# An adaLN block with a spectral filter: the column transform factored into 128 and five points

## The chip, the cores and the metric

The kernel runs on one core of a Trainium2 chip. The metric is device time in microseconds (us) of one execution; the kernel before takes 278.77 us (median of three runs, 278.70 to 280.73). The engines are TensorE (PE; its weight loads are shown apart as PEld), VectorE (DVE), ScalarE (ACT), GpSimd (POOL) and SyncE (SP), whose queue issues nearly all DMAs here.

## The reference

x is 2048 x 640 (bf16, called A_x). w_r and w_i are 2048 x 321, w_mod is 640 x 3840, c is 1 x 640; the feed-forward weights are 640 x 1728 (twice) and 1728 x 640.

```python
mod = (silu(c) @ w_mod).reshape(1, 6, 1, -1)
sa, ca, ga, sb, cb, gb = (mod[:, i] for i in range(6))
h = layernorm(x) * (1 + ca) + sa                  # over the 640 columns, eps 1e-5
X = rfft2(h.astype(float32), axes=(-2, -1))       # 2048 x 321, complex
y = irfft2(X * (w_r + 1j * w_i), s=(2048, 640)).astype(bfloat16)
x = x + ga * y
h = layernorm(x) * (1 + cb) + sb
x = x + gb * ((silu(h @ w_gate) * (h @ w_up)) @ w_down)
```

## The kernel before, in words

Row index s = 16 p + t (p: partition, 128; t: 16 tiles), and frequency k = 128 k2 + k1. All transforms are matmuls with tables (R for the columns, G for the 128 points of the rows, K for the 16 points over t; H, K, Rinv back). The order of the work is written out by hand; each engine runs its instructions in program order and waits on semaphores.

**Stage 1** (lines 270 to 416), for each tile t, in the order of the string `plan`: row statistics on VectorE (`ln1_half`, L280; `ln1_aggr`, L283), the root on ScalarE (L251) and its reciprocal (L289), `ln1_xn` (the normalised row, L293); `turn`, five transposes of 128 columns, even columns, odd columns and a mixed block (L301); `turned`, the copy to SBUF as hT (L305); `dfwd`, 2 x 3 matmuls of 328 columns with the table Rs = R(1 + ca), for even and odd columns (L309); `zcopy` (L318); `s1`, four matmuls of 328 columns with the G table (L332, L333); `acopy` to A_sb (L343), laid out in groups of four column frequencies, so that one group is 128 wide (t, complex part, four frequencies). The evictions are dealt out to VectorE and ScalarE by the lists HT_DVE, Z_DVE and A_DVE.

**Stage 2** (lines 419 to 609) runs over 11 units of four groups. Each group is turned so that (t, part, four) lies on the partitions: the first three units by TensorE (`t2`), the others by a DMA transpose that SP issues (`transposed`). Then `stage_a`, the 16-point transform, combines the even and odd halves E and O into the frequency l and its mirror 320 - l (L463, L464), with an eviction to X (L466) and an add of the transform of sa at row frequency 0 on GpSimd (L469); `product` with the weights Wb and the mirrored Wq (L479); `stage_b`, a transpose by matmul that also adds the two complex products (L488); `evict_y` (L496, L498); `stage_c`, the inverse 16 points (L512, L513), evicted to Ep (L519). The weights of the mirrored frequencies are read through a DRAM scratch tensor, Wneg, which turns the row order; `negate` makes the negative planes on VectorE (L360). `epx` and the fold of the gate ga into Rinv (L586) stand between the units.

**Stage 3** (lines 666 to 712), for each t: `s1inv`, ten matmuls of 128 columns (L673 to L679); the copies to VT (L681, L682); `dinv`, six matmuls of 320 columns with Rinv (L689), and x1 = x + that, two adds of 320 columns on VectorE (L692). Statistics and normalisation of the first four tiles for the second layernorm run between them.

**Feed-forward part** (from L720), four blocks of 512 rows: 13 x 10 matmuls of 512 columns and a rest (`gu13`), Silu on ScalarE (L741), product on VectorE (L742), then the product with w_down (L770, L775) and the output. The fold of gb into w_down (L751) runs in the first block.

Of the kernel before, what the change touches and what calls it, by code (L numbers as in the profile page):

```python
# [18 lines left out]
LH = 164  # L19
L = 2 * LH  # L20
NG = 41
LP = 2 * NG
LW = 324
NC5 = 5
NFC = 14
# [3 lines left out]

_ROWS = np.concatenate([np.arange(0, 512, 2), np.arange(512, 640), np.arange(1, 512, 2)])


# [3 lines left out]
def _tables():  # L41
# [3 lines left out]
    l = np.arange(161, dtype=np.float64)[None, :]  # L45
    ang = 2.0 * np.pi * ((_ROWS[:, None] * l) % D) / D
    R = np.zeros((D, 2, LH))
    R[:, 0, 0:161] = np.cos(ang)
    R[:, 1, 0:161] = np.where(l == 0, 0.0, -np.sin(ang))
    R = R.reshape(NC5, P, L)  # L50
    even = np.arange(P)[:, None] % 2 == 0
    R6 = np.stack([R[0], R[1], np.where(even, R[2], 0.0), np.where(even, 0.0, R[2]), R[3], R[4]])
    T["R"] = np.ascontiguousarray(R6.transpose(1, 0, 2)).astype(_NPBF)
    p = np.arange(P, dtype=np.float64)[:, None]
    k1 = np.arange(128, dtype=np.float64)[None, :]
    G = np.zeros((P, NT, 3, 128))
    for t in range(NT):
        a = 2.0 * np.pi * ((k1 * (16 * p + t)) % S) / S
        G[:, t, 0, :] = np.cos(a)
        G[:, t, 1, :] = -np.sin(a)  # L60
        G[:, t, 2, :] = np.sin(a)
    T["G"] = G.astype(_NPBF)
    kk = np.arange(128, dtype=np.float64)[:, None]
    pp = np.arange(P, dtype=np.float64)[None, :]
    H = np.zeros((128, NT, 3, P))
    for t in range(NT):
        a = 2.0 * np.pi * ((kk * (16 * pp + t)) % S) / S
        H[:, t, 0, :] = np.cos(a)
        H[:, t, 1, :] = np.sin(a)
        H[:, t, 2, :] = -np.sin(a)  # L70
    T["H"] = H.astype(_NPBF)

    F16 = np.exp(-2j * np.pi * np.outer(np.arange(16), np.arange(16)) / 16)

    def fwd(F, turn):
        M = np.zeros((16, 2, 4, 2, 16, 4))
        for j in range(4):
            i = 3 - j if turn else j
            M[:, 0, j, 0, :, i] = F.real
            M[:, 1, j, 0, :, i] = -F.imag  # L80
            M[:, 0, j, 1, :, i] = F.imag
            M[:, 1, j, 1, :, i] = F.real
        return M.reshape(128, 128)

# [51 lines left out]
def adaln_block_kernel(  # L136
# [85 lines left out]
    for i in range(2):  # L222
        nc.sync.dma_start(Wq[:, i], Wneg[i])
# [626 lines left out]
```

## Time and profile before

| | us |
|---|---|
| median of 3 runs | 278.77 |
| the profiled execution's own time | 279.14 |
| its span, first to last instruction | 277.4 |
| TensorE busy | 267.5 (96%) |
| VectorE busy | 162.6 (59%) |
| ScalarE busy | 112.7 (41%) |
| GpSimd busy | 8.9 (3%) |
| granted TensorE clock, mean | 0.998 |

Matmuls are pipelined, and a busy TensorE is not one at its peak. A group's mean is the duration of one instruction; where instructions follow each other without a wait, their starts lie closer together than their durations. The idle time of an engine that is not the bottleneck costs nothing.

### The profile page before, as it was taken

Reading aid. Unit: us, or ns where it says so; the run is one execution under the profiler, and the core shown is the slowest. Engines: PE = TensorE matmul, PEld = TensorE weight load, DVE = VectorE, ACT = ScalarE, POOL = GpSimd, SP = SyncE. Lnnn points to the kernel's source line nnn. Section 1 sums busy time; section 2 is a strip of 40 time slices with the busy share of each in tenths; the row PEclk is TensorE's granted clock in tenths of the full one; section 3 lists DMA queues with packets and bytes.
Section 4 is the critical chain, followed back from the end, with each engine's and each line's share of the span. In section 5 each row is a group of like instructions: output and inputs, shape, how many; then the busy total and the mean of one; then the engine's idle time right before and its main releaser. Section 6 shows DMA issues by size and latency. Waiting matters only on the chain.

```text
span 277.4 us, 5268 instructions
## 1 busy us (share of the span) xinstructions
PE 267.5 (96%) x2120; PEld 168.3 (61%) x2120; DVE 162.6 (59%) x411; ACT 112.7 (41%) x220; POOL 8.9 (3%) x31
## 2 busy tenths in 40 slices
PE   6899989999899999999999999999999999999995
PEld 5667768998687844446654445664444764444663
DVE  4899966799499738876327854224872242432132
ACT  5899666999454662322022233004233103223000
POOL 1000013311000000000000000000000000000000
PEclk9999999999999999999999999999999999999999
DMA  7989999699994200050110050021013011000011
GB/s 260 413 225 211 355 324 194 186 266 397 363 381 95 39 21 24 0 97 0 50 52 16 0 94 3 1 72 33 9 26 70 1 71 35 11 0 0 2 47 47
DMA packets 41034, 31.16 MB, mean 112 GB/s; under 512 B 29361, under 2 KB 37810, under 8 KB 40882
## 3 DMA queue, kind: packets, MB, share of 16 engines
q1 hardware_dynamic: 41008, 30.83, 39.3%
q8 instruction: 16, 0.26, 0.4%
q14 instruction: 8, 0.07, 0.1%
q10 hardware_dynamic: 2, 0.00, 0.0%
HBM read 22.96 MB, written 3.93 MB: 97 GB/s over the span
## 4 chain that ended last, share of the span: by engine, by line
PE 86%; DVE 7%; DMA 2%; ACT 2%; issue 1%; SPq 0%; ACTq 0%; DVEq 0%
PE gps L738 20%; PE ups L738 20%; PE oa L775 10%; PE ob L775 10%; PE zps L309 3%; PE yps L488 3%; DMA Rp<-tab_R 2%; PE xps L463 2%; PE oa L689 2%; PE xps L464 2%; PE gu L725 2%; DVE st L280 2%; PE ob L689 1%; DVE x_sb L692 1%; PE t1ps L301 1%; PE aps L332 1%
## 5 line engine op out<-in xcount | busy, mean ns | idle before, releaser
L738 PE MATMUL gps<-h2T_all,Wg 128*128 128x512 bf16 x260 | 64.6, 379 | 0.0
L738 PE MATMUL ups<-h2T_all,Wu 128*128 128x512 bf16 x260 | 64.6, 379 | 0.0
L741 ACT ACTIVATE sg<-gps 128x512 f32<-128x512 f32 x52 | 31.0, 597 | 74.0 <-PE gps L738 72.3
L738 PEld LDWEIGHTS <-Wu 128*128 128x128 bf16 x260 | 25.4, 98 | 30.7
L738 PEld LDWEIGHTS <-Wg 128*128 128x128 bf16 x260 | 25.4, 98 | 30.5
L742 DVE TENSOR_TENSOR ATb<-ups,sg 128x512 bf16<-128x512 f32 x26 | 17.9, 690 | 32.0 <-PE ups L738 32.0
L742 DVE TENSOR_TENSOR ATa<-ups,sg 128x512 bf16<-128x512 f32 x26 | 17.9, 688 | 20.4 <-PE ups L738 17.5
L775 PEld LDWEIGHTS <-ATa 128*128 128x128 bf16 x208 | 20.2, 98 | 8.8 <-issue 0.8
L775 PEld LDWEIGHTS <-ATb 128*128 128x128 bf16 x208 | 20.2, 98 | 8.6 <-issue 0.5
L785 DVE TENSOR_TENSOR xo<-oa,x_sb 128x320 bf16<-128x320 f32 x16 | 7.8, 489 | 29.7 <-PE ob L770 22.2
L728 ACT ACTIVATE sg<-gu 64x512 f32<-64x512 f32 x4 | 2.3, 586 | 45.3 <-PE gu L725 45.3
L775 PE MATMUL oa<-Wd_sb,ATa 128*128 128x320 bf16 x104 | 15.6, 299 | 0.0
L775 PE MATMUL oa<-Wd_sb,ATb 128*128 128x320 bf16 x104 | 15.5, 299 | 0.0
L775 PE MATMUL ob<-Wd_sb,ATb 128*128 128x320 bf16 x104 | 15.4, 299 | 0.0
L775 PE MATMUL ob<-Wd_sb,ATa 128*128 128x320 bf16 x104 | 15.4, 299 | 0.0
L309 PE MATMUL zps<-Rs,hT 128*128 128x328 bf16 x90 | 14.8, 303 | 0.2
L280 DVE BATCH_NORM_STATS2 st<-x_sb 128x6 f32<-128x320 bf16 x32 | 13.8, 469 | 0.8 <-DMA x_sb<-in_A_x_dram 0.8
L785 DVE TENSOR_TENSOR xo<-ob,x_sb 128x320 bf16<-128x320 f32 x16 | 7.8, 487 | 10.2 <-PE ob L775 10.2
L681 ACT CAST VT<-va 128x512 bf16<-128x512 f32 x16 | 9.4, 586 | 8.0 <-PE va L677 6.2
L488 PE MATMUL yps<-identb,PP 128*128 128x128 bf16 x162 | 11.5, 219 | 0.6 <-DVE PP L479 0.4
L309 PEld LDWEIGHTS <-hT 128*128 128x128 bf16 x96 | 8.8, 98 | 5.2 <-ACT hT L305 1.0
L466 ACT CAST X<-xps 128x512 bf16<-128x512 f32 (+1 forms) x21 | 11.2, 598 | 1.6 <-PE xps L464 1.6
(207 smaller groups left out, 412.8 us busy)
## 6 DMA issues: line engine op xcount, KB each, us to landing
out_dram<-xo SPq DMA_DIRECT2D x16, 160.0 KB, 1.8
Wg<-in_B_w_gate_dram SPq DMA_DIRECT2D x1, 2080.0 KB, 13.4
Wd_sb<-in_B_w_down_dram SPq DMA_DIRECT2D x1, 2080.0 KB
Wu<-in_B_w_up_dram SPq DMA_DIRECT2D x1, 2080.0 KB, 9.8
x_sb<-in_A_x_dram SPq DMA_DIRECT2D x3, 640.0 KB, 8.3
wm_g<-in_w_mod_dram SPq DMA_DIRECT2D x2, 800.0 KB, 11.6
Gtab<-tab_G SPq DMA_DIRECT2D x4, 384.0 KB, 9.3
Htab<-tab_H SPq DMA_DIRECT2D x1, 1536.0 KB, 7.2
```

What stands on the lines that cost most here:

```text
L280: nc.vector.bn_stats(sts[t][:, h, :], x_sb[:, t, 320 * h:320 * h + 320])
L309: nc.tensor.matmul(zap, lhsT=hTs[t][:, 2 * r + i, :], rhs=Rs[:, 3 * r + i, :], start=(i == 0), stop=(i == 2))
L463: nc.tensor.matmul(xps[:, i, :], lhsT=E, rhs=Ktab[:, h, :], start=True, stop=False)
L466: nc.scalar.copy(X[:, :n].rearrange("p i c k j -> p i (c k j)"), xps[:, :n, :])
L488: nc.tensor.matmul(yps[:, i, :], lhsT=PP[:, i, cp].rearrange("p a k j -> p (a k j)"), rhs=identb[:], start=(cp == 0), stop=(cp == 1))
L681: nc.scalar.copy(VTs[t][:, 0:4, :], va[:])
L689: nc.tensor.matmul(os_[odd][:], lhsT=VT[:, 2 * odd + ci if ci < 2 else 4, :], rhs=Rinv_sb[:, odd, ci, :], start=(ci == 0), stop=(ci == 2))
L738: nc.tensor.matmul(o[:], lhsT=w_[:, c5, fc * 128:(fc + 1) * 128], rhs=h2T[:, :, c5, :], start=(c5 == 0), stop=(c5 == NC5 - 1))
L741: nc.scalar.activation(sg[:], gps[:], ACT.Silu)
L742: nc.vector.tensor_tensor(AT[:, fc, :], ups[:], sg[:], ALU.mult)
L775: nc.tensor.matmul(acc[tl][h][:], lhsT=AT[:, fc, tl * 128:(tl + 1) * 128], rhs=Wd_sb[:, fc, h * 320:(h + 1) * 320], start=(tl < 2 and fc = ...
L785: nc.vector.tensor_tensor(xos[tl][:, h * 320:(h + 1) * 320], acc[tl][h][:], x1[:, t, h * 320:(h + 1) * 320], ALU.add)
```

## The change

The column transform of 640 points is split as d = 5 a + r (a: 128, r: five). Stage 1 now transforms the 128 points a for each r apart, and the five points r are merged into the 16-point stage over t (80 complex points in all). Raw x is turned, not the normalised row. Row sums and row sums of squares come from a matmul of hT with itself and a column of ones (`sums`, `diag`); the mean is put in at the Z eviction (`zcopy` adds rv times the negative mean), 1/std by scaling the G table for that t on GpSimd (`gscale`); `pair` stands for the variance, root and reciprocal of two tiles and their two `gscale`. The order strings and eviction lists of stage 1 become a plain loop.

Stage 2 runs over 16 units of four column frequencies and one of the last frequency. Two units (and the last) are turned by TensorE, the others by DMA transposes of two units each. Each frequency's weights are read as windows of Wb (three of five) and Wq (two of five, read backwards). Seven negations run on GpSimd (six of them inside the loop over units), one on VectorE. `mirror` writes a negative copy of part of Ep. Stage 3 uses five pairs of matmuls and one eviction, five matmuls of 128 columns with Rinv, and one x1 add of 640 columns, whose output order has a step of five; for t = 8, 10, 12, 14 the add is a matmul with the identity and ScalarE copies the result. w_down is loaded after the last use of Ep, into its place; the load of the gates' columns (wm_g) is issued after the first DMA transposes. In the feed-forward part two one-bank PSUM tiles become one two-bank tile.

```diff
-    for i, w_ in ((2, A_w_i), (1, A_w_r)):
-        nc.sync.dma_start(Wb[:, i, :, 0:161], w_.rearrange("(k2 k1) l -> k1 k2 l", k1=P)[:, :, 0:161])
...
+    nc.sync.dma_start(wm_sa, wm_v[:, :, 0:D])
+    nc.sync.dma_start(Ktab[:], K_dram)
+    for pl, w_ in ((0, A_w_i), (1, A_w_r)):
+        nc.sync.dma_start(Wb[:, pl, :, 0:321], w_.rearrange("(k2 k1) l -> k1 k2 l", k1=P))
+    for i in range(2):
+        nc.sync.dma_start(Wq[:, 2 - i], Wneg[i])
...
+        def sums(t):
+            for r in range(NR):
+                nc.tensor.matmul(gram(t), lhsT=hT_all[:, t % HB, r, 0:128], rhs=hT_all[:, t % HB, r, 0:129],
+                                 start=(r == 0), stop=(r == NR - 1))
+        def diag(t):
+            junk = ph1.tile([P, 128], BF16, name="junk", bufs=2)
+            nc.vector.tensor_tensor_reduce(out=junk[:], in0=gram(t)[:, 0:128], in1=identb[:], scale=1.0 / D, scalar=0.0,
+                                           op0=ALU.mult, op1=ALU.add, accum_out=ssq[:, t:t + 1])
+            nc.vector.tensor_single_scalar(negm[:, t:t + 1], gram(t)[:, 128:129], -1.0 / D, ALU.mult)
...
+        def gscale(t):
+            Gss[t] = ph1.tile([P, 3, 128], BF16, name="Gs", bufs=5)
+            nc.gpsimd.tensor_scalar(Gss[t][:, 0:2], Gtab[:, t], rstd1[:, t:t + 1], None, ALU.mult)
+            nc.gpsimd.tensor_scalar(Gss[t][:, 2], Gtab[:, t, 1], rstd1[:, t:t + 1], -1.0, ALU.mult, ALU.mult)
...
+        def zcopy(t):
+            Zs[t] = ph1.tile([P, NR, 128], BF16, name="Z", bufs=4)
+            nc.vector.scalar_tensor_tensor(Zs[t][:].rearrange("p r q -> p (r q)"), rv, negm[:, t:t + 1],
+                                           zs.pop(t)[:].rearrange("p b q -> p (b q)")[:, 0:D], ALU.mult, ALU.add)
+        def s1(t):
+            Z, Gs = Zs.pop(t), Gss.pop(t)
+            apss[t] = ps1.tile([P, 2, 512], F32, name="aps", tag="a", bufs=1)
+            for cc, a, b in ((0, 0, 2), (1, 1, 0)):
+                o = apss[t][:, cc, 0:325].rearrange("p (r l) -> p r l", r=NR)
+                nc.tensor.matmul(o, lhsT=Gs[:, a, :], rhs=Z[:, :, 0:NL], start=True, stop=False)
+                nc.tensor.matmul(o[:, :, 1:64], lhsT=Gs[:, b, :], rhs=Z[:, :, NL:128], start=False, stop=True)
+        def acopy(t):
+            ap = apss.pop(t)
+            o = A_sb[:, :, t, :, :].rearrange("p l t c r -> p c r l")
+            i = ap[:, :, 0:325].rearrange("p c (r l) -> p c r l", r=NR)
...
+                (nc.vector.tensor_copy if t in A_DVE else nc.scalar.copy)(o, i)
+        HT_DVE, A_DVE = [], []
...
+        for t in range(NT + 1):
+            if t < NT:
+                dfwd(t)
+            if t + 3 < NT:
+                turn(t + 3)
+                turned(t + 3)
+            if t >= 1:
+                s1(t - 1)
+                acopy(t - 1)
+            if t < NT:
+                zcopy(t)
+            if t + 2 < NT:
+                sums(t + 2)
+                diag(t + 2)
+                if t % 2 == 1:
+                    pair(t + 1)
+            if t == 13:
+                mod_sa()
+            if t == 14:
+                mod_sahat()
...
+            X = ph2.tile([P, NI, 4], BF16, name="X", bufs=3)
+            nc.scalar.copy(X[:].rearrange("p q (b j) -> p q b j", b=2),
+                           xps[:, :, 0:2 * NI].rearrange("p b (j q) -> p q b j", j=2))
...
+            nc.gpsimd.tensor_tensor(xv, xv, sahat[0:1, :, :, 4 * u:4 * u + 4], ALU.add)
...
+            for part, (n, off) in enumerate(((48, 0), (32, 48))):
+                for cp in range(2):
+                    if part == 0:
+                        w = Wbr[:, 48 * cp:48 * cp + 96, l0:l0 + 4][:, ::-1]
+                    else:
+                        w = Wqr[:, 32 * cp:32 * cp + 64, 61 - l0:65 - l0][:, ::-1, ::-1]
+                    o = PP[:, cp].rearrange("p (c q) j -> p c q j", c=2)[:, :, off:off + n]
+                    xi = X[:, 80 * cp + off:80 * cp + off + n].unsqueeze(1).to_broadcast([P, 2, n, 4])
+                    nc.vector.tensor_tensor(o, xi, w.rearrange("p (c q) j -> p c q j", c=2), ALU.mult)
...
+            for j in range(n):
+                for cp in range(2):
+                    nc.tensor.matmul(yf[:, 128 * j:128 * j + 128], lhsT=PP[:, cp, 0:128] if u == 16 else PP[:, cp, 0:128, j],
+                                     rhs=identb[:], start=(cp == 0), stop=(cp == 1))
...
+            ev = eps_[:, :, 0:2 * NI].rearrange("p b (j c a) -> p c a b j", j=2, c=2)
+            copy = nc.vector.tensor_copy if u in E_DVE else nc.scalar.copy
...
+                copy(Ev[:, :, :, 4 * u - 1:4 * u + 3].rearrange("p c a (b j) -> p c a b j", b=2), ev)
...
+        Y_ACT, E_DVE = (3, 6, 9, 12, 15), ()
...
+        for it in range(NU + 2):
+            if it < NU:
+                product(it)
+            if it + 1 < NU:
+                stage_x(it + 1)
+            if 0 <= it - 1 < NU:
+                stage_y(it - 1)
...
+            if 0 <= it - 2 < NU:
+                stage_e(it - 2)
...
+            if it == 0:
+                negate(16, 32, neg_pool)
+                negate_q(33, 49, neg_pool)
...
+    X1_ACT = (8, 10, 12, 14)
...
+        xv = x1[:, t, :].rearrange("p (a r) -> p r a", r=NR)
+        ov = of.rearrange("p (r a) -> p r a", r=NR)
+        for r in range(NR):
+            o = of[:, 128 * r:128 * r + 128]
+            nc.tensor.matmul(o, lhsT=VT[:, r, :], rhs=Rinv_sb[:, r, :], start=True, stop=t not in X1_ACT)
+            if t in X1_ACT:
+                nc.tensor.matmul(o, lhsT=identb[:], rhs=x1[:, t, r::NR], start=False, stop=True)
+        if t in X1_ACT:
+            nc.scalar.copy(xv, ov)
+        else:
+            nc.vector.tensor_tensor(xv, ov, xv, ALU.add)
...
+    Wd_sb = big.tile([P, NFC, D], BF16, name="Wd_sb", tag="ep")
...
-            gps = ps3.tile([P, 512], F32, name="gps", tag="va")
-            ups = ps3.tile([P, 512], F32, name="ups", tag="vb")
+            gu = v2("gu")
```

## The prediction

> **What bounds the kernel now.** I began with the chain that ended last, cut the span where it changes stage, and asked for busy time in each stretch (columns: from:to and length; busy us and instructions of TensorE, its weight loads, VectorE (DVE), ScalarE (ACT), GpSimd (POOL); granted clock; DMA share; GB/s).
>
> ```profile
> 0.00:8.20 8.20, 5.77 (x76) 5.19 (x77) 3.92 (x16) 4.24 (x9) 0.70 (x6) 1.00 0.77 283
> 8.20:37.60 29.40, 28.50 (x247) 19.35 (x245) 27.18 (x82) 24.83 (x45) 0.00 (x0) 1.00 1.00 303
> 37.60:73.90 36.30, 33.60 (x538) 30.51 (x535) 28.97 (x68) 28.56 (x63) 8.19 (x25) 1.00 1.07 274
> 73.90:97.50 23.60, 23.09 (x282) 19.02 (x282) 19.41 (x51) 13.38 (x35) 0.00 (x0) 1.00 0.62 193
> 97.50:277.40 179.90, 176.55 (x991) 94.22 (x987) 83.16 (x197) 41.73 (x70) 0.00 (x0) 1.00 0.12 30
> ```
>
> From 97.5 on, the feed-forward part, TensorE never waits, and the change leaves its 991 matmuls as they are. The question is when it begins. In the three stretches before it TensorE is the fullest engine, but VectorE and ScalarE are at 80% and more: a cut in matmul columns shortens a stretch only until one of these takes over. The chain (start, length, what) gives the edges:
>
> ```profile
> 1.65 6.43 DMA Rp<-tab_R
> 37.63 0.62 PE mpsB L243 x25
> 73.89 0.22 PE va L673
> 98.64 1.08 PE gps L738 x5
> ```
>
> By the page of the profile alone (TensorE busy 96%) one would credit every column saved. Prices come from the groups and from the timeline of VectorE, where starts show the pitch (two products 0.75 together, two adds 0.41 apart):
>
> ```profile
> L343 DVE CAST A_sb<-aps 128x656 bf16<-128x656 f32 x2 | 1.7, 842 | 0.0
> L353 DVE CAST A_sb<-apsh 128x328 bf16<-128x328 f32 x1 | 0.5, 499 | 0.5 <-PE apsh L333 0.5
> L305 ACT COPY hT<-t1ps 128x640 bf16<-128x640 bf16 x9 | 6.0, 691 | 0.0
> ...
> 45.33 1.21 DVE L479 TENSOR_TENSOR PP<-X,Wq 128x512 bf16<-128x512 bf16 x2
> ...
> 54.13 0.43 DVE L506 CAST Ep<-eps__1133 128x64 bf16<-128x64 f32 x1
> ...
> 68.15 0.75 DVE L479 TENSOR_TENSOR PP<-X,Wb 128x512 bf16<-128x512 bf16 x2
> ```
>
> So VectorE reads PSUM at 1.05 ns a column ((842-499)/328); 640 columns last 0.82 and, queued, cost 0.73 (back-to-back starts lie about 0.09 closer than the durations). ScalarE: 0.70, queued 0.60. A product queued costs 0.37 for 512 columns.
>
> **Stage 1 (to the last A eviction, 38.1 now).** TensorE columns per t fall from 640+1968+1312 to 640+645+640+1280: at 0.056 us per 128 from 1.63 to 1.35 us, 4.5 us over 16 t. But bn_stats, xn and the Z evictions become sums, diag, a per-pair root and an eviction that adds rv*negm on VectorE. What each engine must do per pair of t, at queued prices: ScalarE 2 x (0.60 + 0.60) + 0.3 = 2.7; VectorE 2 x (0.73 + 0.20 + 0.12) + 0.5 = 2.6; TensorE 2.7. These would give 2.7 to 2.9 us a pair, against 3.3 now (s1(3) starts at 16.67 and s1(15) at 36.38: 19.7 us for six pairs). What decides is the order of issue, one chain round the three engines per pair: recip, zcopy 0.82, diag 0.34, turn (its PSUM slot waits for diag) 0.43, s1 0.55, sums 0.38, diag 0.29, negm 0.17, two variance steps 0.32, root 0.35, recip 0.21: 3.86 us (each with about 0.05 for its semaphore), since diag(t+2) stands behind zcopy on VectorE and sums behind s1 on TensorE. diag has no row; the 128-column Y cast is 0.29, and I bound it by 0.2 (bn_aggr) and 0.5. The table Rp shrinks from 492 to 160 KB, but Rs still waits for the w_mod columns (7.9), so the first zcopy, behind rv, starts at 10.6 and diag(3) at 13.2. Six pairs: diag(15) at 36.4; root, the sahat matmuls (30, some 0.9 us, ahead of s1(14) on TensorE's queue) and the last two t bring the last eviction to 41.7: **+3.6 us**. GpSimd scales G: the nearest rows are its select on 128 columns (0.29) and its two-input add on 256 (0.72), so 0.5 to 1.2 per t; up to 1.7 s1 does not notice.
>
> **Stage 2 (product(0) at 41.5, first inverse matmul at 73.9 now).** t2, its copy, stage_x, the X eviction and the sahat add (0.28, 0.6, 0.65, 0.85, 0.3) take 2.7 us after the last A, so product(0) starts at 44.4. That add waits on GpSimd's queue behind the G scaling and the first negation, which waits for Wb; sahat itself comes by two small DMAs on SP behind the Wq loads, about 2 us (u13b's copy 1.9) from 39: in time if the loads are (rival 3). Per unit of four columns: TensorE 3 x 1280 columns, 1.6 us (+0.13 for three groups of mod_cols); its weights now have steps of 8 and 10 bytes (a 4-byte step cost 100 against 98 ns), at worst twice the pitch on ten loads, 2.2, at best nothing, which I take. VectorE: products of 384 and 256 columns twice, 2 x (0.30 + 0.23) = 1.07; Y for 11 of 16 units, 0.50; four mirrors, the Rinv fold and the last unit 0.19 per unit. The Wq window is read backwards; no row shows that: nothing at the least, full single rate (as the 960-column Rinv fold with its stepped operand, 1.15 us) +0.27 at the most; I take 0.14. Six negations inside the loop go to GpSimd, some 4.5 us there by the select row's rate, and the row at 45.33 shows two products taking 1.21 in place of 0.75 while GpSimd's shat ran: 0 to 4.5 us, I take 2.5, 0.16 per unit. Sum 2.06. ScalarE: X and E evictions and a third of Y, 1.5 plus twice whatever the new steps cost. So VectorE sets the pace: 16 x 2.06 = 33.0, then Y, stage_e, E, mirror 3.8: first inverse matmul at 81.2, **+3.7 us** more.
>
> By the Trainium skill (SBUF — State Buffer, Who interferes with whom) a VectorE op with two SBUF inputs and a GpSimd op that reads SBUF exclude each other for a whole instruction; the row at 45.33 agrees. By that rule all six negations would stall products, and the sum would be 2 us later.
>
> **Steps.** Three evictions read or write with a hop at every element: A (2-byte writes 320 B apart), X and E (PSUM reads 640 B apart). Before, runs of four went for nothing (ScalarE's Ep cast 0.59 against 0.58 for Y). The only row with hops at each element is L506: 0.43 us for 64 columns, where 0.24 is due, 4.1 ns a column above a fixed 0.17. Bounds: 0 and +1.9 us per 640 columns. Up to +0.27 ScalarE stays under VectorE in stage 2 and under the chain in stage 1; I take +0.25, on the side of the runs-of-four row because the data still come at one element per column: hidden. Above 0.27 each 0.1 costs 0.2 per unit, 3.2 us in stage 2.
>
> **Stage 3 (24.75 us from the first inverse matmul to the first gps group).** TensorE falls from 1.37 to 0.84 us per t. VectorE evicts x1 with a 10-byte step: between 0.74 (two adds 0.41 apart at a 4-byte step, less one fixed part) and 2.8 (L506); neither is near, I take 1.4, about their geometric mean. VectorE up to t=7: start 1.85, 8 x 1.4, stats 4 x 0.93, recip and xn 1.65: 18.4; x1(9) 19.8; each odd t then 0.38 + 1.4 (its PSUM slot is the one two before): 25.2; affine 0.8, now behind x1(15): first gps group at 26.2, **+1.5**. ScalarE: 16 x 0.6, 4 x1, affine, table: not the bound. Wd now loads when Ep is free, after the last s1inv, some 3 us before the feed-forward part. Its 2080 KB need 10 to 13 us from issue to landing (Wu 9.8, Wg 13.4), the u13b copy and the gate row queue behind it on SP, and the first fold stands in the sixth block, 13 us in: nothing; without that cover 1 to 4 us.
>
> By the Trainium skill (Vector Engine (DVE) Microarchitecture Reference, Measured stream behaviour on trn2) a stream that hops at every element runs at 1.7 to 2.5 ns a column. My estimate from that page for x1 is 1.2 to 1.7 us; no row here shows the 10-byte step. With these the sum would be between 2.4 us less and 3.6 more (12 such evictions stand in stage 3's sum).
>
> **Feed-forward part.** gps and ups now share one two-bank tile: it comes free with the product, not with Silu; the product ends 0.8 after ups and the next use is 2.2 later. +0.2 in all.
>
> **Sum.** 3.6 + 3.7 + 1.5 + 0.2 = 9.0 on the profiled execution's 279.14 (span 277.4 and 1.7 around it): 288.1; the runs' median is 0.4 below it: **288**.
>
> **Rivals.**
> 1. Hops dear (for: L506; against: the runs of four). At +0.6 per eviction ScalarE needs 1.5 + 1.2 = 2.7 a unit (+10) and 2.7 + 1.2 a pair, with 0.4 that its root waits 4.3 (+3): 301. Chance 0.18.
> 2. The other side: steps cost nothing, place x1 and Wq. With x1 at 0.74 t=7 is done at 13.1, ScalarE's 2 us for two t set the rest, stage 3 ends at 20.8 (-5.4); without Wq's and half of GpSimd's and the mirrors' terms a unit takes 1.79 (-4.5): 278, 274 to 282 as those terms go; not slower than before once x1 is under 0.9 us and a unit under 1.9. For: the 4-byte step cost 0.02 in 320 columns (0.507 against 0.488 for the output's add). Against: L506. Chance 0.27: 0.13 faster by over 1%, 0.14 within.
> 3. Loads late: 0.85 MB less (Rp, G) goes ahead of Wneg, but Wb and Wq grow by 2.1 MB, and Ktab (0.73 MB) and wm_sa (0.82) now stand ahead of them. By issue and landing the queue ended G at 17.4, Wneg at 26.0, Wb at 31.9, Wq at 35.0: 8.6 us for Wneg's 320-byte rows, 5.9 for Wb's 322; rows of 512 and 642 bytes cost the same or up to twice that. Wq lands between 39 and 50; product(0) wants it at 44.4. Behind it on SP the first transposed blocks (ten in place of eight; 2.8 to 7.0 us to landing now) can go only after the last A, and stage_x(2) wants them at 46.5. 0 to +6, 291. Chance 0.10.
> 4. On top of 2, stage 1 at its engines' sums, 2.9 a pair (-5.8): 272. Chance 0.08.
> That TensorE's columns do not fall as written has no chance; that it changes nothing where TensorE isn't the bound is the forecast.
>
> **Numbers.** Forecast (281 to 293) 0.37, 0.02 of it within 1%. 1% of this kernel, 2.8 us, is about what a measurement can tell from no change. Faster 0.13 + 0.08 = 0.21, within 0.16, slower 0.35 + 0.18 + 0.10 = 0.63. Range 272 to 304: it leaves out the worst of 1 and the better half of 4.
>
> **What would show it.** After: first product near 44, first inverse matmul near 81, first gps near 107; turn behind diag in stage 1; VectorE over 90% busy in stage 2; L701's x1 near 1.4; ScalarE's A, X and E casts under 0.97. Wrong if x1 is near 0.8 or those casts above 1.1.

## The result, and the profile after

The changed kernel takes 350.31 us (median of four runs, 349.57 to 351.60), the kernel before 279.26 beside it: 1.254 times as long, 95% interval 1.247 to 1.260. The prediction said 288 with a range to 304. The sign was right; the size, 71 us in place of 9, was not.

The same edges that the prediction used, in the profiled executions (us from the start of the span; in brackets the length of the stage):

| | last A eviction | first inverse matmul | first gate group of the feed-forward part | end |
|---|---|---|---|---|
| before | 38.1 | 73.9 (35.8) | 98.6 (24.7) | 277.4 (178.8) |
| predicted | 41.7 | 81.2 (39.5) | 107.4 (26.2) | 286.4 (179.0) |
| after | 79.0 | 125.1 (46.1) | 161.7 (36.6) | 347.8 (186.1) |

So no stage came out as predicted: stage 1 is 40.9 longer than before (3.6 predicted), stage 2 10.3 (3.7), stage 3 11.8 (1.5), the feed-forward part 7.4 (0.2).

The busy time by stage of the kernel after, cut at the last A eviction, the first inverse matmul and the first feed-forward matmul (columns as in the prediction):

```profile
8.20:78.97 70.77, 41.00 (x351) 29.56 (x350) 24.50 (x88) 55.85 (x42) 22.77 (x34) 0.67 0.47 158
78.97:125.12 46.15, 37.97 (x446) 31.24 (x446) 35.54 (x88) 29.73 (x45) 16.96 (x23) 0.87 0.81 234
125.12:159.53 34.41, 23.06 (x286) 21.00 (x287) 27.48 (x32) 19.31 (x23) 0.00 (x0) 0.80 0.25 76
159.53:347.80 188.27, 179.60 (x989) 94.42 (x987) 82.57 (x195) 41.97 (x71) 0.00 (x0) 0.99 0.12 34
```

In stage 1 ScalarE is now the fullest engine, 55.9 of 70.8 us, where TensorE was before with 28.5 of 29.4. And the granted clock, 1.00 in every stage before, is 0.67 there. The groups of the kernel after, with mean duration behind the bar, say what fills ScalarE; the last line, from the kernel before, is its A eviction on ScalarE:

```profile
L312 ACT CAST A_sb<-aps 128x650 bf16<-128x650 f32 x15 | 45.0, 2999 | 10.0 <-PE aps L302 10.0
L701 DVE TENSOR_TENSOR x_sb<-oab,x_sb 128x640 bf16<-128x640 f32 x12 | 22.6, 1942 | 6.7 <-PE oab L695 6.7
L464 ACT CAST X<-xps 128x640 bf16<-128x640 f32 x16 | 11.2, 699 | 5.6 <-PE xps L462 5.6
...
L408 POOL TENSOR_SCALAR Wb<-Wb,neg 128x768 bf16<-128x768 bf16 x3 | 6.6, 2199 | 0.0
...
L343 ACT CAST A_sb<-aps 128x656 bf16<-128x656 f32 x13 | 9.2, 711 | 3.3 <-PE aps L333 3.2
```

One A eviction lasts 3.0 us; the rows of before (L343) had 0.84 on VectorE and 0.71 on ScalarE for 656 columns. The X eviction, which hops 640 bytes at every element too, but in what it reads, lasts 0.70, as any ScalarE copy of 640 columns. The x1 add lasts 1.94 on VectorE, and as a copy on ScalarE (L699) 1.945. GpSimd needs 2.2 us for a negation of 768 columns and 1.6 for one of 512, where the prediction had 0.75 (4.5 for six).

The chain that ended last (start, length, what) through stage 1 of the kernel after, and two later places:

```profile
17.37 3.03 ACT A_sb L312
...
20.44 0.30 PE aps L301
...
21.19 1.61 ACT A_sb L312
...
25.50 3.01 ACT A_sb L312
28.56 0.43 PE aps L301
...
29.83 1.86 ACT A_sb L312
...
84.08 2.01 POOL Wb L408
...
201.08 0.50 DVE xo L796
```

The A evictions and the four matmuls between them set the pace: A has one PSUM tile, so s1 of the next t waits for the eviction, and the eviction for s1. (The 1.61 and 1.86 are pieces of the chain, which passes from there to a root that follows on ScalarE; these two evictions last 2.99 like the others.) The first of the four matmuls takes 0.30 at 20.44 and 0.43 at 28.56, and from one eviction to the next it is 3.8 us in the first round and 4.3 in the others: the granted clock goes up and down within the stage. At 84 the chain runs through GpSimd's negations, at 201 TensorE waits for the output adds.

### The profile page after: what moved, and what is told of

It is laid out like the page before. It is cut to its first block, busy times and chain, and to the rows that moved or that the text cites. A ratio compares the mean times of both kernels' runs of the same rounds, so it can differ in the third digit from the quotient of the medians.

```text
span 347.8 us, 5294 instructions
## 1 busy us (share of the span) xinstructions
PE 287.2 (83%) x2142; PEld 181.4 (52%) x2142; DVE 171.2 (49%) x414; ACT 151.2 (43%) x187; POOL 40.6 (12%) x64
## 4 chain that ended last, share of the span: by engine, by line
PE 65%; ACT 17%; DVE 10%; issue 4%; POOL 3%; DMA 0%; ACTq 0%; DVEq 0%
PE gu L750 31%; PE oa L786 16%; ACT A_sb L312 11%; DVE x_sb L701 4%; PE aps L301 3%; PE aps L302 2%; PE gu L738 2%; DVE xo L796 1%; POOL Wb L408 1%; PE yps L500 1%; PE oab L695 1%; DVE PP L490 1%; PE va L681 1%; PE va L682 1%; ACT Ep L540 1%
## 5 line engine op out<-in xcount | busy, mean ns | idle before, releaser
L753 ACT ACTIVATE sg<-gu 128x512 f32<-128x512 f32 x52 | 31.1, 598 | 79.8 <-PE gu L750 75.1
L750 PE MATMUL gu<-h2T_all,Wg 128*128 128x512 bf16 x260 | 64.9, 380 | 0.4 <-DVE ATa L754 0.4
L750 PE MATMUL gu<-h2T_all,Wu 128*128 128x512 bf16 x260 | 64.6, 379 | 0.0
L312 ACT CAST A_sb<-aps 128x650 bf16<-128x650 f32 x15 | 45.0, 2999 | 10.0 <-PE aps L302 10.0
L750 PEld LDWEIGHTS <-Wg 128*128 128x128 bf16 x260 | 25.5, 98 | 31.7 <-issue 1.9
L750 PEld LDWEIGHTS <-Wu 128*128 128x128 bf16 x260 | 25.5, 98 | 30.6
L754 DVE TENSOR_TENSOR ATb<-gu,sg 128x512 bf16<-128x512 f32 x26 | 17.9, 689 | 33.3 <-ACT sg L753 33.2
L786 PE MATMUL oa<-Wd_sb,ATa 128*128 128x320 bf16 x208 | 29.9, 299 | 2.7 <-DVE xo L796 2.3
L786 PE MATMUL oa<-Wd_sb,ATb 128*128 128x320 bf16 x208 | 29.6, 299 | 2.3 <-DVE xo L796 2.3
L754 DVE TENSOR_TENSOR ATa<-gu,sg 128x512 bf16<-128x512 f32 x26 | 17.8, 686 | 24.1 <-ACT sg L753 24.0
L701 DVE TENSOR_TENSOR x_sb<-oab,x_sb 128x640 bf16<-128x640 f32 x12 | 22.6, 1942 | 6.7 <-PE oab L695 6.7
L282 POOL TENSOR_SCALAR Gs<-Gtab,rstd 128x256 bf16<-128x256 bf16 x16 | 14.8, 926 | 47.7 <-DVE rstd L278 47.7
L695 PE MATMUL oab<-Rinv_sb,VT 128*128 128x128 bf16 x80 | 10.7, 248 | 9.6 <-DVE x_sb L701 5.7
L266 DVE CUSTOM_DVE_ANT_0 junk<-t1ps,identb 128x128 bf16<-128x128 f32 x16 | 4.7, 291 | 26.5 <-PE t1ps L261 22.1
## 6 DMA issues: line engine op xcount, KB each, us to landing
x_sb<-in_A_x_dram SPq DMA_DIRECT2D x3, 640.0 KB, 10.7
```

The source lines that it names most:

```text
L282: nc.gpsimd.tensor_scalar(Gss[t][:, 0:2], Gtab[:, t], rstd1[:, t:t + 1], None, ALU.mult)
L312: (nc.vector.tensor_copy if t in A_DVE else nc.scalar.copy)(o, i)
L695: nc.tensor.matmul(o, lhsT=VT[:, r, :], rhs=Rinv_sb[:, r, :], start=True, stop=t not in X1_ACT)
L701: nc.vector.tensor_tensor(xv, ov, xv, ALU.add)
L750: nc.tensor.matmul(o, lhsT=w_[:, c5, fc * 128:(fc + 1) * 128], rhs=h2T[:, :, c5, :], start=(c5 == 0), stop=(c5 == NC5 - 1))
L753: nc.scalar.activation(sg[:], gu[:, 0, :], ACT.Silu)
```

## The experiments

Five of these kernels ran once: the exchange in the kernel before, the steps, x1, the unread matmuls and the X add on VectorE. Executions of one kernel lie up to 2 us apart here, so for these the stage edges say more than the totals.

### The A evictions, the same elements in another order

```diff
-            o = A_sb[:, :, t, :, :].rearrange("p l c r -> p c r l")
-            i = ap[:, :, 0:325].rearrange("p c (r l) -> p c r l", r=NR)
+            o = A_sb[:, :, t, :, :].rearrange("p l c r -> p c l r")
+            i = ap[:, :, 0:325].rearrange("p c (r l) -> p c l r", r=NR)
```

The loop over r, innermost, now writes neighbours. (The expectation says runs of ten; as the loops stand they are runs of five, 10 bytes.)

> One line: the A eviction walks the same elements in another order, so that its writes come in runs of ten (20 bytes) and its reads of PSUM hop 260 bytes. Theory 1 (each lone 2-byte write costs about 4.4 ns, the read hops cost nothing, as the X eviction's 0.70 us shows): the eviction falls from 3.0 to 0.7-0.9 us, the pitch per t in stage 1 from 4.2 to 2.0-2.3, the last A eviction from 79 to 43-48, and the granted clock in stage 1 returns above 0.9 because TensorE is busy again; total 311-318. Rival (the price is not the lone write but the distance of 320 bytes between rows of A, or reading two PSUM banks with TensorE beside it): the eviction stays above 2 us and the total above 335. Rival on the clock (it falls for another reason than idle TensorE): clock stays at 0.5-0.7 though the eviction is short.

Measured: 314.54 us, 1.124 times before (1.120 to 1.128), as theory 1 had it. 35.8 us of the 71 are gone with these two lines. The groups, the windows of stage 1 and the chain of one pair of t in this kernel:

```profile
L312 ACT CAST A_sb<-aps 128x650 bf16<-128x650 f32 x15 | 13.2, 881 | 2.3 <-PE aps L302 2.3
```

```profile
8.20:44.25 36.05, 28.79 (x367) 22.84 (x365) 22.98 (x91) 25.48 (x42) 21.21 (x34) 0.95 0.92 309
```

```profile
22.34 0.29 DVE junk L266
...
23.14 0.30 ACT rstd L216
...
23.63 0.78 DVE Z L293
...
25.77 0.31 PE t1ps L261 x5
...
26.21 0.29 DVE junk L266
```

The eviction is 0.88 (0.69 is due for 640 contiguous columns, as the steps below show; why runs of five cost 0.18 more here stays open), the last one ends at 44.3, the clock in stage 1 is 0.95. And from one diag (junk, L266) to that of the next pair it is 26.21 - 22.34 = 3.87 us, through the very steps that the prediction listed (root, reciprocal, Z eviction, diag, turn, s1, sums, diag) for 3.86. That step was right; it was buried under the evictions.

### The exchange in the kernel before

```diff
-                A_sb[:, :, t, :, :].rearrange("p l c j -> p c l j"),
-                apss.pop(t)[:, :, :L].rearrange("p c (l j) -> p c l j", j=4))
+                A_sb[:, :, t, :, :].rearrange("p l c j -> p c j l"),
+                apss.pop(t)[:, :, :L].rearrange("p c (l j) -> p c j l", j=4))
```

> The kernel before, with the two loops of its A evictions exchanged: the same elements go to the same places, but each write is a lone 2 bytes, 256 bytes from the last, in place of runs of four. Theory 1: its fourteen evictions of 656 columns rise from 0.71 (ScalarE) and 0.84 (VectorE) to about 2.9 us, PSUM for A has one buffer there too, so most of 14 x 2.1 = 29 us shows: 300-310, and the granted clock, 1.00 until now, falls in stage 1. Rival (the order of writes is nothing by itself, it is the new layout): 279.

Measured: 316.85, against 279.77. The group of ScalarE's and that of VectorE's evictions, then the window of stage 1:

```profile
L343 ACT CAST A_sb<-aps 128x656 bf16<-128x656 f32 x13 | 40.1, 3082 | 10.8 <-PE aps L333 10.8
L343 DVE CAST A_sb<-aps 128x656 bf16<-128x656 f32 x2 | 6.2, 3076 | 1.1 <-PE aps L333 1.1
```

```profile
8.20:74.00 65.80, 39.48 (x264) 24.82 (x261) 31.94 (x81) 54.05 (x45) 0.00 (x0) 0.76 0.49 151
```

Nothing but the order of the elements is different (the writes are now lone, and the reads hop 16 bytes, which the next run shows to be free), no byte lands elsewhere, and 36 of the 37 us appear in stage 1, which ends at 74 in place of 38. Both engines take 3.08 us, and the granted clock falls to 0.76 in a stage where it had been 1.00. The total is 7 us above the upper end of what was expected; that counted 2.1 us for each of fourteen evictions, where fifteen take 2.2 to 2.4 more, and nothing for the clock.

### The price of a step, by itself

> Does none of the reference's work, it copies x to the output; it measures the price of one eviction of 640 columns by itself. VectorE first, then ScalarE, one line each, four times: bf16 writes from PSUM at a step of 1, 2, 3, 4, 5, 8, 16 elements, at 160 (as A), the same in runs of ten (160 apart), runs of 2, 4 and 5 at a distance of 16, reads with a hop, runs of four that start at an odd or an even place, 4-byte writes contiguous and at a step of 5, an SBUF read at a step of 5, the forms of the x1 add. Theory 1: lone 2-byte writes of any step from 2 up cost 2.8-4.6 ns a column on both engines, growing with the step until each element has its own line, runs of four or more cost under 1.3 ns, hopping reads nothing. Rival: only steps of 16 and more are dear, and x1's 1.94 comes from the hop of its second operand. Negation of 512 columns on GpSimd about 1.5 us, on VectorE 0.3-0.6.

```diff
+    for _ in range(N):
+        nc.vector.tensor_copy(line(wide, 5), pf)
...
+    for _ in range(N):
+        nc.vector.tensor_copy(far(wide), farsrc(pf))
+    for _ in range(N):
+        nc.vector.tensor_copy(far_runs(wide), farsrc_runs(pf))
```

Each form ran four times in a row, first on VectorE, then on ScalarE. The groups of VectorE, by line: bf16 writes at a step of 1, 2, 3, 5 and 8 elements (L71 to L81) and at A's 160 (L85); at 160 in runs of ten (L87); in runs of two at a distance of 16 (L89); 4-byte writes at a step of five (L105); the x1 add of the changed kernel (L115); the last line is ScalarE at 160:

```profile
L71 DVE CAST wide<-ps 128x640 bf16<-128x640 f32 x4 | 3.3, 824 | 0.1
L73 DVE CAST wide<-ps 128x640 bf16<-128x640 f32 x4 | 3.5, 867 | 0.1
L75 DVE CAST wide<-ps 128x640 bf16<-128x640 f32 x4 | 4.9, 1220 | 0.1
...
L79 DVE CAST wide<-ps 128x640 bf16<-128x640 f32 x4 | 7.7, 1925 | 0.1
L81 DVE CAST wide<-ps 128x640 bf16<-128x640 f32 x4 | 11.9, 2984 | 0.1
...
L85 DVE CAST wide<-ps 128x640 bf16<-128x640 f32 x4 | 11.7, 2932 | 0.1
L87 DVE CAST wide<-ps 128x640 bf16<-128x640 f32 x4 | 3.3, 825 | 0.1
L89 DVE CAST wide<-ps 128x640 bf16<-128x640 f32 x4 | 3.3, 826 | 0.1
...
L105 DVE COPY w<-ps 128x640 f32<-128x640 f32 x4 | 5.2, 1294 | 0.1
...
L115 DVE TENSOR_TENSOR cont<-ps,src 128x640 bf16<-128x640 f32 x4 | 7.7, 1925 | 0.1
...
L134 ACT CAST wideA<-ps 128x640 bf16<-128x640 f32 x4 | 11.7, 2932 | 0.1
```

What is to be seen: a step of two costs little (867 in place of 824; on ScalarE 868 in place of 692), from three to eight each element of step adds 0.35 us per 640 columns ((1925 - 1220) / 2), and from 16 bytes on it is level at 2.8 to 3.0 us (2826 at a step of 16), 4.4 to 4.7 ns a column. Two neighbours are enough to be near full speed again: runs of two that start 32 bytes apart take 826 on VectorE and 732 on ScalarE, runs of ten that start 320 bytes apart 825 and 693. ScalarE's numbers for lone writes are the same to 2 ns (1220, 1926 and 2986 ns at 3, 5 and 8; 2932 at 160), though its contiguous 640 columns take 0.69: so it is not the engine's own pace, it is the writing of lone 2-byte elements. 4-byte elements at a step of five cost less than half of the added price (1294). The x1 add that hops in its second operand alone took 852 ns; with a hop in the result alone it is 1926, with both 1925: the result is what costs. Runs of four that begin at an odd place, as half of the E eviction's do, took 0.496 against 0.426 for 320 columns on ScalarE; that is some 0.07 for E, which measures 0.97 to 1.05 in the kernel where 0.70 is due, and the rest of its excess stays open. GpSimd's negation of 512 columns took 1.49 with nothing beside it, VectorE's 0.29.

### x1 in natural column order

```diff
-        xv = x1[:, t, :].rearrange("p (a r) -> p r a", r=NR)
-        ov = of.rearrange("p (r a) -> p r a", r=NR)
+        xv = x1[:, t, :].rearrange("p (a r) -> p a r", r=NR)
+        ov = of.rearrange("p (r a) -> p a r", r=NR)
```

> The x1 add and the four x1 copies walk the same elements in natural column order: writes and the second operand contiguous, PSUM reads hop 512 bytes. Theory 1: 1.94 falls to about 0.8 on both engines; stage 3 (34.4 us from first inverse matmul to the feed-forward part) loses 8-12 us, then ScalarE's VT copies are next; total 338-342. Rival (the 1.94 comes from PSUM, or from the second operand): stays at 1.9 and the total within 1% of 350.

Measured: 339.88, 10.4 less than after. The group of the adds and the window of stage 3 (ScalarE's four copies, L699, are 0.69 there):

```profile
L701 DVE TENSOR_TENSOR x_sb<-oab,x_sb 128x640 bf16<-128x640 f32 x12 | 9.6, 805 | 7.5 <-PE oab L695 7.5
```

```profile
127.80:150.87 23.07, 20.15 (x286) 18.20 (x287) 15.50 (x32) 14.62 (x23) 0.00 (x0) 0.93 0.25 64
```

Stage 3 is 11.3 us shorter (34.41 before this edit) and so about as long as it was before the change (23.65 from the first inverse matmul to the first of the feed-forward part, 73.89 to 97.54).

### What the low clock costs by itself

```diff
+            for _ in range(10):
+                nc.tensor.matmul(zs[t][:, 1, 128:512], lhsT=identb[:], rhs=Rs[:, 0:3, :].rearrange("p r q -> p (r q)"),
+                                 start=True, stop=True)
```

> The changed kernel, its A evictions as they are, plus ten matmuls of 384 columns per t into an unused part of the Z tile's PSUM (their results are not read), so that TensorE is never idle in stage 1. It tells what the low granted clock costs by itself. Theory (the evictions set the pace, and the clock falls because TensorE idles behind them): the clock in stage 1 stays near 1.0, the four s1 matmuls between two A evictions take 0.55-0.65 in place of 1.25 us, the last A eviction comes 6-10 us earlier than 79, total 340-345. Rival 1 (the low clock is the main cost of stage 1): 20 us or more go. Rival 2 (the clock falls whatever TensorE does): nothing changes, 350.

Measured: 348.08, 2.2 less than after's median and 1.5 less than its fastest execution, where 340 to 345 was expected; the last A eviction at 78.1, 0.9 earlier and not 6 to 10. The window of stage 1 and the chain of one t:

```profile
16.00:76.00 60.00, 47.71 (x458) 33.67 (x457) 20.91 (x76) 52.94 (x36) 18.66 (x30) 0.99 0.43 137
```

```profile
29.00 3.03 ACT A_sb L315
...
32.83 2.49 ACT A_sb L315
```

The clock is 0.99, and every round from one A eviction to the next takes 3.8 us (7.65 a pair), where nine of the fourteen rounds in the kernel after took 4.3. From the first A eviction to the fifteenth it is 53.6 us (17.55 to 71.13), in the kernel after 57.9 (13.57 to 71.51): the low clock costs 4.4 us in stage 1. Nearly all of it is lost again, because the added matmuls put off the first A eviction by 4.0 us, which the expectation had forgotten. The clock is a consequence: busy TensorE brings it back, and the 3.0 us evictions remain.

### Four repairs at once, read by stage

The A and x1 orders above, all negations on VectorE, and one-bank PSUM tiles in the feed-forward part:

```diff
-        negate(0, 16, neg_pool)
+        negate(0, 16, neg_dve)
...
-            gu = v2("gu")
-            for w_, o in ((Wg, gu[:, 0, :]), (Wu, gu[:, 1, :])):
+            gps, ups = one("gps", "va"), one("ups", "vb")
+            for w_, o in ((Wg, gps[:]), (Wu, ups[:])):
...
-        acc = [(o2, o2, v2, v2)[tl]("oa") for tl in range(4)]
+        acc = [[one("oab", "vo"[tl < 2] + "ab"[h]) for h in range(2)] for tl in range(4)]
```

> Four repairs in one kernel, one per stage, read by the stages' edges: A evictions in runs of ten (stage 1, as in the run that did that alone), all negations on VectorE in place of GpSimd (stage 2), x1 in natural column order (stage 3), one-bank PSUM tiles in the feed-forward part as before the change. Expected against the run with the A evictions alone (314.5; last A eviction 44.3, first inverse matmul 90.9, first feed-forward matmul 124.8, span 313.5): stage 1 as there; stage 2 from 46.6 to 36-39, because the X add no longer stands behind 2 to 4 us of negation on GpSimd and no product waits beside one (VectorE pays 7 x 0.3-0.5 for them); stage 3 from 34 to 21-25; feed-forward part from 188.7 to 179-181. Total 285-293. Rival for stage 2 (GpSimd is not what holds it, VectorE's own sum is): 44 or more. Rival for the feed-forward part (its extra comes from the fold of w_down that arrives late, not from the tiles): 184 or more there.

Measured: 292.54, 1.046 times before (1.042 to 1.050). The windows by stage:

```profile
44.44:86.34 41.90, 35.08 (x445) 28.77 (x445) 35.11 (x95) 29.51 (x45) 6.03 (x17) 0.96 0.96 249
86.34:110.14 23.80, 20.18 (x285) 18.21 (x286) 15.74 (x32) 15.30 (x25) 0.00 (x0) 0.93 0.32 96
110.14:291.70 181.56, 178.34 (x989) 94.78 (x988) 82.55 (x195) 41.70 (x69) 0.00 (x0) 0.99 0.14 39
```

Stage 3 came as expected (23.8) and the feed-forward part nearly (181.6 against 188.7; 179 to 181 expected), and a block of the feed-forward part is again 44.0 us, as before, in place of 45.6. Stage 2 went from 46.6 to 41.9, not to the 36 to 39 expected: the negations cost VectorE 3.1 us, and the fold of ga into Rinv, reached earlier, now waits 1.15 us for the gate row.

That shares out the 71 us: 35.8 are the A evictions with the low clock that they bring, 10.4 the x1 writes (by their own run), 11.6, as what is left, the negations and the two-bank tiles together (57.8 in all by this run, of it 4.7 in stage 2 and 7.1 in the feed-forward part against the run with the A evictions alone). What is left against before, by the same edges, is 6.3 in stage 1, 6.1 in stage 2, 1.0 in stage 3 and 0.9 in the feed-forward part: 14.3 in all, where the prediction summed 3.6, 3.7, 1.5 and 0.2, which is 9.0. So even without its dear terms, and with the negations moved, stages 1 and 2 are each some 2.5 us over their sums.

### GpSimd's negations: its queue, or the port that it shares?

The four repairs, but the negations on GpSimd again and the X add on VectorE:

```diff
-            nc.gpsimd.tensor_tensor(xv, xv, sahat[0:1, :, :, 4 * u:4 * u + 4], ALU.add)
+            nc.vector.tensor_tensor(xv, xv, sahat[0:1, :, :, 4 * u:4 * u + 4], ALU.add)
```

> The four repairs but with the negations on GpSimd again, as in the change, and the X add of 40 values moved to VectorE, so that it no longer stands behind them in GpSimd's queue. Tells apart why GpSimd's negations cost time in stage 2 (46.6 us from the last A eviction to the first inverse matmul with them, 42.2 with VectorE doing them in 2.5 us). Queue theory (the X add waits behind 2 to 4 us of negation, products wait for X 4.2 us in all): stage 2 at 39-41, total 289-291. Sharing theory (a product that runs beside a negation takes about 1.0 us longer, five times in that trace): 44-46, total 294-297.

Measured: 293.77, stage 2 from 44.3 to 86.8: 42.5, between the two. The groups of this kernel, then those of the run with four repairs:

```profile
L490 DVE TENSOR_TENSOR PP<-X,Wq 128x256 bf16<-128x256 bf16 x32 | 11.3, 390 | 0.0
L490 DVE TENSOR_TENSOR PP<-X,Wb 128x384 bf16<-128x384 bf16 x32 | 10.3, 360 | 0.2
L408 POOL TENSOR_SCALAR Wq<-Wq,neg 128x512 bf16<-128x512 bf16 x3 | 6.8, 2257 | 0.0
L467 DVE TENSOR_TENSOR X<-X,sahat 1x40 bf16<-1x40 bf16 x16 | 2.9, 182 | 4.2 <-ACT X L464 4.2
```

```profile
L490 DVE TENSOR_TENSOR PP<-X,Wq 128x256 bf16<-128x256 bf16 x32 | 10.5, 370 | 0.0
L490 DVE TENSOR_TENSOR PP<-X,Wb 128x384 bf16<-128x384 bf16 x32 | 9.9, 350 | 2.0 <-POOL X L467 1.7
```

All products together are 21.6 us long beside GpSimd's negations and 20.4 without them: sharing costs 1.2 in this kernel, and it lengthens the negations too (Wq 2.26; 1.49 with nothing beside it). Against the run with the A evictions alone, stage 2 differs only in where the X add runs, and it is 4.1 us shorter (46.6 to 42.5) although the X adds now cost VectorE 2.9 us, which the expectation had not counted. Not all of the 4.1 is the queue: in that run the products took 23.3, so 1.7 of them went too. But VectorE's idle time in stage 2 fell from 10.7 to 6.9 us while its busy time hardly changed (35.9, 35.5). So waiting behind GpSimd's queue was the larger part and the longer products the smaller; how the two share the 4.7 us exactly stays open.

### The order of issue in stage 1

The prediction's fourth rival had stage 1 at its engines' sums, 2.9 us a pair. Three orders on top of the four repairs. First, sums and diag of t+2 ahead of everything else of the round:

```diff
         for t in range(NT + 1):
+            if t + 2 < NT:
+                sums(t + 2)
+                diag(t + 2)
+                if t % 2 == 1:
+                    pair(t + 1)
             if t < NT:
                 dfwd(t)
```

> The four repairs and one more: in stage 1 the row sums and their diagonal of t+2 are issued ahead of the column transform of t in place of behind the Z eviction. By the prediction's step (one chain of 3.86 us per pair round three engines, because diag stands behind the Z eviction) a pair falls to 2.9-3.1, the last A eviction from 44.3 to 37-40, all else as with four repairs: 5-7 us less. Rival (VectorE, ScalarE or GpSimd by its 2.6 us per pair is already the bound, or the latency only moves to root and G scaling): less than 2 us.

Measured: 294.48, 1.9 more than without it, where 5 to 7 less was expected; a pair takes 4.2 us, because sums now waits for the copy to hT of the same round (0.7) and the transposes behind it for the sums. Second, the same lines behind the copy to hT:

```diff
                 turned(t + 3)
+            if t + 2 < NT:
+                sums(t + 2)
+                diag(t + 2)
+                if t % 2 == 1:
+                    pair(t + 1)
             if t >= 1:
                 s1(t - 1)
```

> The four repairs, with the row sums and their diagonal of t+2 issued behind the transposes of t+3 and ahead of s1 (in the run before they stood ahead of everything, and there the sums waited for a copy to hT of the same round, which made a new loop of 1.9 us per t: copy 0.7, sums, column transform, transposes). Here they wait only for the copy of the round before. Theory (the prediction's: the order of issue sets the pair's 3.9 us, because diag stands behind the Z eviction): the pair falls to ScalarE's sum, 2 x (0.60 + 0.82) + 0.3 = 3.1-3.3, the last A eviction from 44.2 to 39-41, total 287.5-290. Rival (another loop of the same length, through root, reciprocal and G scaling on GpSimd, 0.7 + 2.6 us, holds it): 291-294.

Measured: 292.39, no difference from 292.54, as the rival had it: a pair is 3.9 us again, on a chain diag, variance, root, reciprocal, Z eviction, s1, column transform, transposes, sums. Third, reciprocal and G scaling of the pair behind the Z eviction of the round:

```diff
             root(t, t + 2)
-            recip(t, t + 2)
-            gscale(t)
-            gscale(t + 1)
+            if t == 0:
+                scale(0)
...
                 zcopy(t)
+            if t % 2 == 1 and t + 2 < NT:
+                scale(t + 1)
```

> The order of the run with 292.4 (sums ahead of s1), with one more move: reciprocal and G scaling of a pair stand behind the Z eviction of the same round, so that VectorE does not hold the Z eviction back while ScalarE takes the root. In both orders tried so far the trace shows one loop per pair through every engine: diag 0.4, two variance steps 0.4, root 0.3, reciprocal 0.2, Z eviction 0.8, s1 0.7, column transform, transposes and sums 0.9: 3.9 us. Theory (that loop sets the pace, and taking root and reciprocal out of it leaves 2.8, under ScalarE's sum of 3.1): pair at 3.1-3.3, the last A eviction from 44.1 to 38.5-40.5, total 286-289. Rival (another loop takes over, through the later G scaling on GpSimd, 2.6 us per pair, to s1): pair still at 3.7 or more, 290-293.

Measured: 290.81, 1.042 times before (1.038 to 1.047); last A eviction at 42.6 in place of 44.1, a pair 3.7 us, at the rival's end of what was expected. The chain of two pairs in this kernel:

```profile
20.50 0.29 DVE junk L266
...
21.37 0.79 DVE Z L293
...
25.19 0.29 ACT rstd L216
25.48 0.74 ACT A_sb L312
...
27.02 0.92 ACT A_sb L312
...
27.98 0.29 DVE junk L266
```

Now one round goes by way of Z and the next by way of root and two A evictions, which wait for each other through A's one PSUM tile: 27.98 - 20.50 is two pairs. Taking a wait out let the next one, hardly shorter, set the pace. What order would reach 2.9 is open; with two tiles for A it might, but PSUM is full in this stage, and it was not tried.

### Three smaller repairs

On top of the second order: the fold of ga four units later, the affine of the first tiles spread over rounds 10 to 14 of stage 3, and added matmuls (not read) from t = 8 on.

```diff
-        if t == 14:
-            ln2_affine(0, (0, 1))
-        if t == 15:
-            ln2_affine(0, (2, 3, 4))
+        if t in (10, 11, 12, 13, 14):
+            ln2_affine(0, (t - 10,))
...
+        if t >= 8:
+            for _ in range(3):
+                nc.tensor.matmul(va[:, 1, 128:512], lhsT=identb[:], rhs=Htab[:, 0:2, :, :].rearrange("p a b q -> p (a b q)")[:, 0:384],
+                                 start=True, stop=True)
```

> That kernel and three more edits: the fold of ga into Rinv four units later (with four repairs VectorE stood 1.2 us before it, waiting for the gate row's way through DRAM), the affine of the first four tiles spread over rounds 10 to 14 of stage 3 in place of behind its end, and three matmuls of 384 columns per round from t = 8 on into an unused part of a PSUM tile (not read), so that the granted clock is full when the feed-forward part begins (its first 15 matmuls took 4.0 in place of 3.2 us). Expected 1.0 + 1.0 to 1.5 + 0.8 to 1.5 less than the run beside it: 283.5-287. So the changed kernel with all repairs stays slower than the kernel before (279.7), by its longer stage 2. Rival: the affine's place is taken by the last x1 add, and only 1 us or less goes.

Measured: 292.44, no difference from 292.39. The feed-forward part lost 1.5 us (178.7 from its first gate group, by the clock), and stage 3 grew by more: 112.0 - 84.8 = 27.2 against 25.5. What grew it is the added matmuls: the chain through the last rounds runs through them, one row like this in every round:

```profile
106.20 0.49 PE va L687 x3
```

They make up 10.8% of the chain in these 27.2 us, some 2.9 us, and TensorE is busy for 24.8 us of the stage in place of 21.7. The 1.5 us of affine at the end of the chain, which the edit was to take away, are gone from it. Stage 2, where the fold was moved, is 0.2 shorter, not 1.0. None of these kernels beats the kernel before.

## Why the prediction was wrong, by its own steps

**Steps (the failing one).** "I take +0.25, on the side of the runs-of-four row": the A eviction measured 2.3 us more than a plain copy, nine times the term, and more than the upper bound of 1.9. X and E stood under the same term; X cost nothing and E some 0.3: the prediction put writes and reads into one line, and only lone writes are dear. The right row was on the table. L506, 4.1 ns a column, was a lone write at a wide step, and its price is the one that the step table shows for both engines (4.4 to 4.7); the runs-of-four row, which I preferred, tells nothing of lone elements, since two neighbours already make the difference. Then the range did not hold its own bound: rival 1 ("hops dear") was priced at +0.6, 301 us, not at +1.9. With 2.6 us per A eviction ScalarE's part of a pair is 2 x (0.60 + 2.6) + 0.3 = 6.7 against the chain's 3.86, some 21 us over stage 1 from the prediction's own rows. Measured at full clock it is 7.65 a pair: with one PSUM tile for A, the eviction (3.0) and s1 (0.8) run one behind the other, a wait that the prediction did not name. What no row of before could show is the clock: with TensorE idle behind the evictions it fell to 0.67 and added about 4.

By the Trainium skill (SBUF — State Buffer, Specifications (TRN2)) SBUF has lines of 16 bytes and wants two accesses per line: the level from a step of eight bf16 on and the free runs of two agree (2.98, 0.83 us); a step of three, with more than two per line, does not (1.22). The page of the Trainium skill that the prediction cited for 1.7 to 2.5 ns a column (Vector Engine (DVE) Microarchitecture Reference, Measured stream behaviour on trn2) states its figures for 32-bit streams. The 4-byte row here, 2.0 ns, agrees with it; 2-byte writes, 3.0 from a step of five and 4.4 to 4.7 from eight, do not follow it, and I had used it for bf16.

**Stage 1.** The chain of 3.86 us per pair was right (3.87 measured once the evictions were short), the last A eviction at 44.3 in place of 41.7: the pairs began 1.3 later (first diag of the chain at 14.5, not 13.2), and the two halves of the last eviction run one behind the other. (TensorE's columns, at the 0.056 us per 128 that the prediction gives, come to 1.72 and 1.40 us, not 1.63 and 1.35; the sum does not use them.)

**Stage 2.** Products a little under the prediction (1.08 to 1.12 us per unit at queued pitch; 1.07 + 0.14), the last product to the first inverse matmul as predicted (3.7; 3.8). Wrong: GpSimd's negations, sized at 4.5 us for six by the select row, take 11.6 for six in the loop and 2.2 for the one ahead of it, and the sum let them only share a port with the products. What they do first is stand in GpSimd's queue ahead of the X adds. The queue was named for the first negation and forgotten for the others.

**Stage 3.** x1 taken as 1.4, between 0.74 and 2.8; 1.94 measured: a term mis-sized inside its bounds. Over the twelve adds on VectorE that is 6.5 of the 10.4 us by which the stage exceeds its forecast; the rest, with four such copies on ScalarE and a clock of 0.80, is not shared out. Rival 2's 20.8 us for an x1 at 0.74 was too low as well: with 0.81 the stage takes 24.3 to 26.0 in the kernels without added matmuls.

**Feed-forward part.** "+0.2 in all" looked at the gate and up tiles alone. The output tiles became two-bank tiles too, and each next pair of output groups waits for both adds (0.56 twice a block, as at 201.06, of the 1.6 that a block is longer); in the first block, where VectorE is late with folds and statistics, TensorE waits for it at 179.8 and 192.5, 0.4 and 0.3 us; and the part begins at a low clock (2.16 us for five matmuls that take 1.08).

**Loads late** (rival 3) did not show: in the run with short A evictions the first product, at 47.2, waited for the X add, not for Wb or Wq.

## What to carry to other kernels

Look at the innermost loop of every eviction's output: lone 2-byte writes take 1.93 us per 640 columns when they lie 10 bytes apart and 2.8 to 3.0 from 16 bytes on, on VectorE and ScalarE alike, where runs of two or more take 0.83 and 0.69 to 0.73; the order in which 4-byte values were read from PSUM was free. If source and destination disagree, hop in the read. And when a cost has no row, put its upper bound through the chain as carefully as the value you take: here the bound alone would have made ScalarE the pace of stage 1. An instruction moved to an idle engine stands in that engine's queue; ask what small instruction behind it is on the path.

## What the runs showed of the hardware

The price of a lone 2-byte write is the same on two engines of different pace (1.93 us at a step of five, 2.93 at 160, to within 2 ns), and rises by 0.35 us per 640 columns and element of step between 2 and 8. The granted clock fell to a mean of 0.67, and in the exchange in the kernel before to 0.76, in a stage where TensorE waited for each A eviction (in the kernel after s1's weight loads stood 24.0 us in 14 places, 3.3 at the longest), and was back at 0.99 when unread matmuls filled the pauses. GpSimd takes 2.9 us per 1000 columns for a multiply by a constant (1.49 for 512, alone), five times VectorE's (0.29).
